# Eight weight loads instead of eleven, the last twelve row blocks of a projection multiplied straight into the next stage's layout, and two closing copies without a shared bank: one decode step of attention and MLP on one core

## The chip, the cores and the metric

The kernel runs on one core of one Trainium2 chip. The metric is the time of one execution in microseconds of device time; the time before is the median of three runs, 190.84 us (190.77 to 190.88). One more execution was recorded by the hardware profiler, and all views of the profile come from that one.

## What is computed

One token passes through two layers. The reference, cut to what matters here:

```
h  = x + A(layernorm(x), k_cache, v_cache, wq, wo)     # x: 1x1x512
out = h + B(layernorm(h), w1, w2, w3, w4)

A: q = x @ wq                       # 32 query heads of 128, 8 key/value heads, 16384 cached positions
   p = softmax(q k^T / sqrt(128));  o = p v;  return o.reshape(1, 1, 4096) @ wo     # wo: 4096x512
B: h = gelu(layernorm(x) @ w1), shifted along the sequence by one or two places, @ w2
   x1 = x + hs                      # with one token the shifted h is all zeros: x1 = x
   return x1 + gelu(layernorm(x1) @ w3) @ w4            # w3: 512x1792, w4: 1792x512
```

Everything is bfloat16. The cache is 64 MB of keys and values, and wq, wo, w3 and w4 are another 11.9 MB; w1 and w2 don't matter, since the shifted branch is zero for a sequence of one.

## The kernel before, in words

The program is written as a list of operations with the tiles that each reads and writes (class Program); semaphore waits follow from that list. Besides, an operation may name a PSUM bank (argument `bank`): then it waits for the last user of that bank on any other engine, even where no data passes between them (line 63). Instructions of one engine keep the order in which they are written.

**The attention** (lines 665 to 682) goes through four pairs of key/value heads. For each pair SyncE issues two loads of 4 MB of keys into the two halves of tile kb and one load of 8 MB of values into vb (two of 4 MB for the last pair). VectorE transposes the keys, TensorE multiplies them with the query, VectorE, ScalarE and TensorE do the softmax, and TensorE multiplies with the values (line 636), four column groups of 32 side by side. The result of a pair is 32 rows of tile o_m.

**The weights behind it** (lines 685 to 693) are loaded by the same SyncE queue in pieces, each with a semaphore of its own. The lists WO, W3 and W4 (lines 329 to 332) say which blocks go together: wo's 32 row blocks in four loads, w3's four in three, w4's fourteen in four. wo goes into the first half of kb, w3 and w4 into the second, so the loads are issued when the last keys there have been transposed, and lie in the queue behind the last values.

**The stages behind the attention** are one chain:

- Lines 696 and 698 (VectorE): o_m is summed into o_f and cast to o_b, 128 partitions by 32 row blocks. The cast waits for the first load of wo.
- Line 702 (TensorE): 32 matmuls, one for each row block of wo, 512 columns each. Four of them run side by side in four column groups of the array and add up in one bank, so the result is four partial rows of 512, each copied over 32 partitions.
- Line 706 (VectorE): the copy osum of that bank into SBUF. Line 708 (TensorE): four fp32 matmuls (two passes each) add up the four partial rows and put quarter q of the row on partitions 32q to 32q+31. This is the "row's layout": four quarters of 128 values, each copied on 32 partitions.
- row_sums (lines 479 to 495): line 483 adds the residual x, held in tile hx since the start, and takes the sum; line 489 the sum of squares, line 491 the transposed row, line 493 (TensorE) the mean over the partitions, line 495 copies it to st.
- Line 714 (ScalarE): hc, the row less its mean in bfloat16. It also waits for the first load of w3.
- Line 720 (TensorE): 16 matmuls with w3. variance (lines 497 to 511), line 724 and line 725 meanwhile give the scales and xsum, the residual of the second layer.
- Lines 729 and 733: for each half of the 14 blocks, the gelu (ScalarE) and a transpose into hcol (VectorE).
- Lines 737 to 751 (TensorE): 14 blocks m of w4, four matmuls each, side by side, all into one bank. In the middle (line 740) four fp32 matmuls with an identity add xsum. A block waits for its load and its half of hcol.
- Line 752 (ScalarE) copies partitions 0 to 63 of the result into fin, line 754 (VectorE) partitions 64 to 127; both name the bank "mn". SyncE sends the row out (line 755) and waits for it (line 757).

**Branches**: TensorE's program is kept short: loops run over the pairs and pieces (method _tensor), and behind them the instructions stand in a row. `pe(None)` and `dve(None)` mark a place where the program branches on a condition that is never true (lines 150 and 314), with a prefetch hint given at the program's start. In the kernel before, TensorE's stands ahead of block 10 of w4.

Of the kernel before, what the change touches and what calls it, by code (L numbers as in the profile page):

```python
# [9 lines left out]
ALU = mybir.AluOpType  # L10
# [308 lines left out]
D = 512  # L319
# [6 lines left out]
NCH = D // 128  # L326
FQ = FM // 4
NHC = FM // 128
WO = ((0, 12), (12, 24), (24, 30), (30, 32))
VP = 2  # L330
W3 = ((0, 2), (2, 3), (3, 4))
W4 = ((0, 5), (5, 10), (10, 13), (13, 14))
BLOCK = (0, 2, 1, 3)
PAIRS = HKV // 2
RPARTS = 9
# [7 lines left out]
def bass_sequential_preLN__gqa_block_cached__mixer_s_mlp__decode_kernel(  # L343
# [13 lines left out]
    with ExitStack() as ctx:  # L357
# [16 lines left out]
        x4 = sb("x4", [4, 128], BF16)  # L374
        mean4 = sb("mean4", [128, 128], FP32)
        ident_f = sb("ident_f", [128, 128], FP32)
        ident = sb("ident", [4, 4], BF16)
        quarter = sb("quarter", [4, 4, 32], BF16)
# [23 lines left out]
        osum = sb("osum", [128, D], FP32)  # L402
# [3 lines left out]
        o_b = sb("o_b", [128, 32], BF16)  # L406
        hr = sb("hr", [128, 128], FP32)
        hx = sb("hx", [128, 128], FP32)
        rs = [sb(f"rs{i}", [128, 2], FP32) for i in range(2)]
        hc = sb("hc", [128, NCH, 32], BF16)  # L410
        xs = sb("xs", [128, 128], FP32)
        xsum = sb("xsum", [128, 128], FP32)
# [3 lines left out]
        fin = sb("fin", [64, 256], BF16)  # L416
# [4 lines left out]
        wq_sb, wo_sb = vb, kb[0]  # L421
# [3 lines left out]
        banks = ps("banks", [128, 8, 512], FP32)  # L425
        s_ps = banks[:, 0:2, :]
        row = banks[:, :, :].rearrange("p b f -> p (b f)")
        O_ps = [banks[:, 2, :], banks[:, 3, :]]
        A_ps, mn_ps = banks[:, 4, :], banks[:, 5, :]
        m_ps, n_ps = mn_ps[:, 0:256], mn_ps[:, 256:512]  # L430


        def load(name, dst, src, key, by="SP", also=()):
            P.op(by, lambda e: e.dma_start(dst, src), w=[key, *also], dma=name)  # L434
# [24 lines left out]
        def dve(fn, r=(), w=(), bank=()):  # L459
            return P.op("DVE", fn, r, w, bank)  # L460

        def act(fn, r=(), w=(), bank=()):
            return P.op("ACT", fn, r, w, bank)
# [4 lines left out]
        def pe(fn, r=(), w=(), bank=(), also=()):  # L468

            return P.op("PE", fn, r, w, bank, also=also)  # L470

        def piece(cuts, m):
            return [lo <= m < hi for lo, hi in cuts].index(True)

        def copies(col, n):

            return col.to_broadcast([col.shape[0], n])

        def row_sums(i, row, key):

            h, hk = (hr, "hr") if i else (hx, "hx")
            if i:
                dve(lambda e: e.scalar_tensor_tensor(h[:, :], row[:, 0:128], 1.0, hx[:, :], ALU.mult, ALU.add,
                                                     accum_out=rs[i][:, 0:1]),
                    r=[key, "hx"], w=[hk, ("rs", i, 0)], bank=[key])
            else:
                dve(lambda e: e.tensor_scalar(h[:, :], row[:, 0:128], 0.0, 0.0, ALU.add, ALU.add,
                                              accum_out=rs[i][:, 0:1]), r=[key], w=[hk, ("rs", i, 0)], bank=[key])
            dve(lambda e: e.scalar_tensor_tensor(xs[:, :], h[:, :], 1.0, h[:, :], ALU.mult, ALU.mult,
                                                 accum_out=rs[i][:, 1:2]), r=[hk], w=["xs", ("rs", i, 1)])  # L490
            dve(lambda e: e.transpose(hT[:, :, :].rearrange("p k u -> p (k u)"),
                                      h[:, :].rearrange("p (i k) -> p k i", k=NCH)), r=[hk], w=["hT"])
            pe(lambda e: e.matmul(n_ps[:, 0:2], mean4[:, :], rs[i][:, :], start=True, stop=True),
               r=[("rs", i, 0), ("rs", i, 1), "mean4"], w=["n"], bank=["mn"])
            dve(lambda e: e.tensor_copy(st[i][:, 0:2], n_ps[:, 0:2]), r=["n"], w=[(("st", i), 0)], bank=["mn"])

        def variance(i):
# [7 lines left out]
            for n in range(1 + i):  # L505
# [22 lines left out]
            r=["ident", "x4"], w=["quarter"])  # L528
        pe(lambda e: e.matmul(O_ps[0][:, 0:128], quarter[:, :, :].rearrange("p q u -> p (q u)"), x4[:, :],
                              start=True, stop=True), r=["quarter"], w=[("O", 0)], bank=[("O", 0)])  # L530
        row_sums(0, O_ps[0], ("O", 0))
        variance(0)
        act(lambda e: e.activation(scr[0:1, 0:1], mean4[0:1, 0:1], ACTF.Exp), r=["mean4"], w=["scr"])
# [4 lines left out]
            r=["ident_f"], w=["row32"])  # L538
        dve(lambda e: e.tensor_reduce(maskdd[:, :], ident_f[:, :].rearrange("p (n d) -> p d n", d=4), AX.X, ALU.add),
            r=["ident_f"], w=["maskdd"])  # L540
# [6 lines left out]
        for z, m, key, mk in ((zo, rowgh, "zo", "rowgh"), (zd, maskgh, "zd", "maskgh")):  # L547
# [5 lines left out]
            r=["hT", (("st", 0), 0), (("st", 0), 6)] + [("v", x) for x in range(VP)], w=["xn"])  # L553
# [3 lines left out]
        for i, key in enumerate(keys):  # L557
            P.part("query", i)
            for k in range(NCH):
                pe(lambda e, k=k: e.matmul(row[:, bass.ds(P.b, 512)], copies(xn[:, k:k + 1], 128),  # L560
                                           wq_k[:, k, bass.ds(P.c, REP * DH)], start=(k == 0), stop=(k == NCH - 1)),
                   r=["xn"], also=[("v", x) for x in range(VP)], w=["n" if key == "mn" else key], bank=[key])
        P.part()
        for g in range(2):
            half = banks[64 * g:64 * g + 64, PAIRS * g:PAIRS * g + PAIRS, :].rearrange("p j c -> p (j c)")
            for b in range(2):
# [3 lines left out]
                    r=["n" if x == "mn" else x for x in keys[PAIRS * g:PAIRS * g + PAIRS]], w=["qcol"],  # L570
                    bank=keys[PAIRS * g:PAIRS * g + PAIRS])
# [112 lines left out]
        act(lambda e: e.activation(scr[0:1, 1:2], mean4[0:1, 0:1], ACTF.Gelu_apprx_tanh), r=["mean4"], w=["scr"])  # L684
        for n, (lo, hi) in enumerate(WO):
            load(f"wo{n}", wo_sb[:, lo * D:hi * D], A_wo.rearrange("(p r) c -> p (r c)", p=128)[:, lo * D:hi * D],
                 ("r", 0, n))
        w3_in = B_w3.rearrange("(p k) f -> p k f", p=128)
        for n, (lo, hi) in enumerate(W3):
            load(f"w3{n}", w3_sb[:, lo:hi, :], w3_in[:, lo:hi, :], ("r", 1, n))  # L690
        w4_in = B_w4.rearrange("(p m) c -> p m c", p=128)
        for n, (lo, hi) in enumerate(W4):
            load(f"w4{n}", w4_sb[:, lo:hi, :], w4_in[:, lo:hi, :], ("r", 1, len(W3) + n))


        dve(lambda e: e.tensor_reduce(o_f[:, :], o_m[:, :, :].rearrange("p d r -> p r d"), AX.X, ALU.add),
            r=["o_m"], w=["o_f"])
        dve(lambda e: e.tensor_copy(o_b[:, :], o_f[:, :]), r=["o_f", ("r", 0, 0)], w=["o_b"])

        for r_ in range(32):  # L700
            q = r_ % 4
            pe(lambda e, r_=r_, q=q: e.matmul(O_ps[0][32 * q:32 * q + 32, :], copies(o_b[:, r_:r_ + 1], 32),  # L702
                                              wo_sb[:, r_ * D:(r_ + 1) * D], start=(r_ < 4), stop=(r_ >= 28)),
               r=["o_b"] + [("r", 0, n) for n in (piece(WO, r_),) if n], w=[("O", 0)], bank=[("O", 0)])
        h_ps, hkey = banks[:, 6, :], "spare0"
        dve(lambda e: e.tensor_copy(osum[:, :], O_ps[0][:, :]), r=[("O", 0)], w=["osum"], bank=[("O", 0)])
        for q in range(4):
            pe(lambda e, q=q: e.matmul(h_ps[32 * q:32 * q + 32, 0:128], copies(row32[:, 0:1], 32),
                                       osum[:, q * 128:(q + 1) * 128], start=True, stop=True),
               r=["osum", "row32"], w=[hkey], bank=[hkey])  # L710
        s = st[1]
        S = ("st", 1)
        row_sums(1, h_ps, hkey)
        act(lambda e: e.activation(hc[:, :, :], hT[:, :, :], ACTF.Identity, bias=s[:, 0:1], scale=1.0),
            r=["hT", (S, 0)] + [("r", 1, 0)], w=["hc"])


        for k in range(NCH):
            for q in range(4):
                pe(lambda e, k=k, q=q: e.matmul(s_ps[32 * q:32 * q + 32, 0, 0:FQ], hc[:, k, :],  # L720
                                                w3_sb[:, k, q * FQ:(q + 1) * FQ], start=(k == 0), stop=(k == NCH - 1)),
                   r=["hc"] + [("r", 1, n) for n in (piece(W3, k),) if n], w=[("s", 0)], bank=[("s", 0)])
        variance(1)
        dve(lambda e: e.tensor_scalar(xs[:, :], hr[:, :], s[:, 0:1], None, ALU.add), r=["hr", (S, 0)], w=["xs"])
        dve(lambda e: e.scalar_tensor_tensor(xsum[:, :], xs[:, :], s[:, 6:7], hr[:, :], ALU.mult, ALU.add),
            r=["hr", "xs", (S, 6)], w=["xsum"])
        for n in range(2):
# [6 lines left out]
                hcol[:, lo:hi, :].rearrange("p m u -> p (m u)"),  # L734
                hg[:, :].rearrange("p (i m) -> p m i", m=NHC)[:, lo:hi, :]), r=[("hg", n)], w=[("hcol", n)])
        dve(None)
        for m in range(NHC):
            if m == NHC // 2:
                for o in range(4):
                    pe(lambda e, o=o: e.matmul(  # L740
                        n_ps[32 * o:32 * o + 32, 0:128], ident_f[:, 32 * BLOCK[o]:32 * BLOCK[o] + 32], xsum[:, :],
                        start=False, stop=False, skip_group_check=True),
                       r=["ident_f", "xsum"], w=["n"], bank=["mn"])
            if m == W4[-2][0]:
                pe(None)
            for o in range(4):
                pe(lambda e, m=m, o=o: e.matmul(  # L747
                    n_ps[32 * o:32 * o + 32, 0:128], hcol[:, m, :], w4_sb[:, m, BLOCK[o] * 128:(BLOCK[o] + 1) * 128],
                    start=(m == 0), stop=(m == NHC - 1),
                    skip_group_check=True),  # L750
                   r=[("hcol", 2 * m // NHC), ("r", 1, len(W3) + piece(W4, m))], w=["n"], bank=["mn"])
        act(lambda e: e.activation(fin[:, 0:128], n_ps[0:64, 0:128], ACTF.Identity),  # L752
            r=["n"], w=[("fin", 0)], bank=["mn"])
        dve(lambda e: e.tensor_copy(fin[:, 128:256], n_ps[64:128, 0:128]), r=["n"], w=[("fin", 1)], bank=["mn"])  # L754
        P.op("SP", lambda e: e.dma_start(out[0, 0:1, :].rearrange("o (q j) -> (o q) j", q=2), fin[31:33, :]),
             r=[("fin", 0), ("fin", 1)], w=["out"], dma="out")
        P.op("SP", lambda e: e.nop(), r=["out"])
# [31 lines left out]
```

## Time and profile before

| | |
|---|---|
| median of three runs | 190.84 us (190.77 to 190.88) |
| the profiled execution's own time | 191.29 us |
| its span, first to last instruction | 189.7 us |
| mean granted TensorE clock | 0.823 |
| busy: TensorE matmuls, weight loads, VectorE, ScalarE, GpSimd | 116.1, 45.8, 115.4, 9.3, 5.7 us |
| read from HBM | 79.17 MB, 417 GB/s over the span |

The span leaves out 1.6 us around the program's instructions. In the profile PE is TensorE's matmuls, PEld its weight loads, DVE VectorE, ACT ScalarE, POOL GpSimd, SP SyncE; a name with q (SPq) is an instruction of the engine's sequencer, such as the issue of a DMA. Times in the views are microseconds from the span's start. "128*32 128x512" means a weight of 128 rows and 32 columns against 512 moving columns.

### The profile page before, as it was taken

What the parts mean: (1) busy time and instruction counts of PE and PEld (TensorE: products, weight loads), DVE (VectorE), ACT (ScalarE), POOL (GpSimd) and SP (SyncE); (2) the same over time, 40 slices, a digit from 0 to 9 for tenths busy, and PEclk for the clock granted to TensorE, in tenths of its full rate; (3) what the DMA queues carried; (4) which work ended last, traced back from release to release, by engine and by line L of the source; (5) the groups of instructions that cost most, each with busy time, mean ns of one, the idle gap of its engine ahead of it and who ended that gap; (6) DMA issues with size and microseconds to landing.
All of it is one profiled execution on the core that took longest, in us unless ns stands there. A gap on an engine that the chain in (4) does not pass through costs nothing.

```text
span 189.7 us, 2177 instructions
## 1 busy us (share of the span) xinstructions
PE 116.1 (61%) x701; PEld 45.8 (24%) x701; DVE 115.4 (61%) x140; ACT 9.3 (5%) x16; POOL 5.7 (3%) x10
## 2 busy tenths in 40 slices
PE   1009709997194498950842999606539996094544
PEld 1004203442031143320310343202213432041113
DVE  4900799995514998945047989460469896604151
ACT  3000000000200000002000000020000000500020
POOL 1900000000000000000000000000000000000010
PEclk9999985999858589995597599975975999759955
DMA  6999999999899999997999998999999999999992
GB/s 221 442 435 442 442 442 449 442 442 442 380 435 408 435 553 428 442 442 339 435 428 422 477 401 387 442 442 435 442 442 442 428 428 415 422 402 416 411 411 106
DMA packets 3613, 79.19 MB, mean 417 GB/s; under 512 B 410, under 2 KB 540, under 8 KB 1564
## 3 DMA queue, kind: packets, MB, share of 16 engines
q1 hardware_dynamic: 3604, 79.17, 97.5%
q8 instruction: 1, 0.02, 0.0%
q10 hardware_dynamic: 8, 0.00, 0.0%
HBM read 79.17 MB, written 0.00 MB: 417 GB/s over the span
## 4 chain that ended last, share of the span: by engine, by line
DMA 66%; DVE 15%; PE 14%; issue 3%; SPq 1%; ACT 0%; DVEq 0%
DMA kb<-in_A_k_cache_dram 46%; DMA kb<-in_B_w_dram 14%; DVE kt L583 13%; PE banks L600 8%; DMA vb<-in_A_wq_dram 7%; PE banks L560 4%; SPq L434 1%; DVE qcol L567 1%; PE banks L594 1%; PE banks L747 1%; DVE qb L574 0%; PE banks L740 0%; DVE xn L551 0%; DVE fin L754 0%; ACT fin L752 0%
## 5 line engine op out<-in xcount | busy, mean ns | idle before, releaser
L583 DVE STREAM_TRANSPOSE kt<-kb 128x2048 int32<-128x2048 int32 (+1 forms) x37 | 71.3, 1988 | 5.8 <-DMA kb<-in_A_k_cache_dram 4.2
L600 PE MATMUL banks<-kt,qn 128*128 x256 | 69.8, 422 | 0.2
L600 PEld LDWEIGHTS banks<-kt,qn 128*128 x256 | 26.6, 104 | 41.9 <-issue 25.1
L636 PE MATMUL banks<-vb,pt 128*32 128x512 bf16 x256 | 22.8, 534 | 2.8 <-POOLq L449 2.8
L652 DVE TENSOR_SCALAR od<-banks,rowc 128x128 f32<-128x128 f32 x4 | 1.4, 351 | 24.7 <-PE banks L636 24.7
L594 PE MATMUL banks<-qn 128*128 128x512 bf16 x8 | 3.9, 494 | 18.4 <-DVE kt L583 18.4
L560 PE MATMUL banks<-vb,xn 128*128 x32 | 8.4, 428 | 10.1 <-DVE xn L551 10.1
L625 DVE STREAM_TRANSPOSE pt<-p_sb 64x1024 bf16<-64x1024 bf16 x8 | 9.9, 1239 | 5.4 <-ACT p_sb L621 5.3
L636 PEld LDWEIGHTS banks<-vb,pt 128*32 128x32 bf16 x256 | 8.6, 130 | 15.2 <-issue 10.3
L621 ACT ACTIVATE p_sb<-banks,bias 128x1024 bf16<-128x1024 f32 x4 | 4.5, 1114 | 155.8 <-DVE nmh L617 155.8
L643 PE MATMUL banks<-acc,zd 128*32 128x1 f32 x8 | 1.1, 203 | 17.7 <-DVE pt L625 17.7
L610 DVE TENSOR_REDUCE mx<-banks 128x1 f32<-128x1024 f32 x4 | 4.9, 1224 | 8.1 <-PE banks L600 8.1
L567 DVE STREAM_TRANSPOSE qcol<-banks 64x1024 f32<-64x1024 f32 x4 | 4.8, 1226 | 6.4 <-PE banks L560 6.4
L560 PEld LDWEIGHTS banks<-vb,xn 128*128 128x128 bf16 x32 | 3.5, 108 | 14.6 <-issue 11.8
L509 POOL TENSOR_TENSOR st<-st,expo 128x1 f32<-128x1 f32 (+1 forms) x2 | 1.3, 630 | 176.1 <-DVE st L507 176.1
L613 PE MATMUL banks<-mxd,mean 128*128 128x128 f32 x8 | 2.0, 326 | 6.6 <-DVE mxd L611 6.6
L594 PEld LDWEIGHTS banks<-qn 128*128 128x128 bf16 x8 | 0.8, 100 | 20.8 <-issue 20.5
L658 PE MATMUL banks<-od,zo 128*32 128x128 f32 x8 | 1.6, 284 | 6.5 <-DVE od L655 6.5
L643 PEld LDWEIGHTS banks<-acc,zd 128*32 128x32 f32 x8 | 0.7, 140 | 18.4 <-DVE pt L625 18.4
L655 DVE SCALAR_TENSOR_TENSOR od<-banks,rowc,od 128x128 f32<-128x128 f32 x12 | 4.2, 351 | 0.4
L702 PE MATMUL banks<-kb,o_b 128*32 128x512 bf16 x32 | 2.7, 384 | 2.4 <-DMA kb<-in_A_wo_dram 1.3
L548 DVE COPY zo<-rowgh 128x32 f32<-128x32 f32 x1 | 3.6, 3627 | 0.0
(71 smaller groups left out, 42.4 us busy)
## 6 DMA issues: line engine op xcount, KB each, us to landing
kb<-in_A_k_cache_dram SPq DMA_DIRECT2D x8, 4096.0 KB, 29.7
vb<-in_A_v_cache_dram SPq DMA_DIRECT2D x2, 4096.0 KB, 29.6
vb<-in_A_wq_dram SPq DMA_DIRECT2D x1, 4096.0 KB, 12.6
kb<-in_A_wo_dram SPq DMA_DIRECT2D x2, 1536.0 KB, 25.4
kb<-in_B_w_dram SPq DMA_DIRECT2D x2, 640.0 KB, 25.4
kb<-in_B_w_dram SPq DMA_DIRECT2D x1, 896.0 KB, 22.4
kb<-in_B_w_dram SPq DMA_DIRECT2D x2, 448.0 KB, 23.4
kb<-in_A_wo_dram SPq DMA_DIRECT2D x1, 768.0 KB, 28.5
```

Of the source, the lines that this page charges most:

```text
L548: dve(lambda e, z=z, m=m: e.tensor_copy(z[:, :].rearrange("p (n d) -> p n d", d=4), m[:, :, :].rearrange("p g h -> p (g h)").unsqueeze(2). ...
L560: pe(lambda e, k=k: e.matmul(row[:, bass.ds(P.b, 512)], copies(xn[:, k:k + 1], 128), wq_k[:, k, bass.ds(P.c, REP * DH)], start=(k == 0), s ...
L567: dve(lambda e, g=g, b=b, half=half: e.transpose(qcol[64 * g:64 * g + 64, 2 * b:2 * b + 2, :, :].rearrange("p e m u -> p (e m u)"), half.r ...
L583: P.op("DVE", lambda e, view=view: e.transpose(view(kt), view(kb[y])), r=[("r", y, i) for i in range(RPARTS)], w=[("kt", t + i) for i in r ...
L594: pe(lambda e: e.matmul(row[:, bass.ds(P.y, 512)], copies(none, 128), copies(none, 512), start=True, stop=False, skip_group_check=True), r ...
L600: pe(lambda e, n=n: e.matmul(row[:, bass.ds(P.y, 512)], qn[:, n, bass.ds(P.q, 128)], key_piece(P.k, n), start=False, stop=(n == 3), skip_g ...
L610: dve(lambda e: e.tensor_reduce(mx[:, :], s_all, AX.X, ALU.max), r=[("s", 0), ("s", 1)], w=["mx"], **both)
L621: act(lambda e: e.activation(p_sb[:, :], s_all, ACTF.Exp, bias=bias[:, 0:1], scale=float(SCALE), accum_out=acc[:, :]), r=[("s", 0), ("s", ...
L625: dve(lambda e, g=g: e.transpose(pt[64 * g:64 * g + 64, :, :, g, :], p_sb[64 * g:64 * g + 64, :]), r=["p"], w=["pt"])
L636: pe(lambda e, l=l, ct=ct, ch=ch: e.matmul(O_ps[0][32 * ct:32 * ct + 32, :], pt[:, l, ch, :, :].rearrange("p g u -> p (g u)"), tiles[:, l ...
L655: dve(lambda e, block=block, c=c: e.scalar_tensor_tensor(od[:, :], block, rowc[:, c:c + 1], od[:, :], ALU.mult, ALU.add), r=[key, "rowc", ...
L702: pe(lambda e, r_=r_, q=q: e.matmul(O_ps[0][32 * q:32 * q + 32, :], copies(o_b[:, r_:r_ + 1], 32), wo_sb[:, r_ * D:(r_ + 1) * D], start=(r ...
```

## The change

- WO, W3 and W4 are cut into three, two and three loads: eight in place of eleven. The first load of wo holds 20 row blocks, the first of w3 three of its four, the first of w4 eight of fourteen.
- Only the first 20 row blocks (`near`) are multiplied by line 702's form and go through osum. The other twelve are multiplied straight into the row's layout: four matmuls of 128 columns each (function direct), one for each quarter, into the bank where osum's four partial rows are added.
- The residual x enters that bank first, by one matmul with `quarter` and x4, as at the start of the kernel; row_sums no longer adds hx.
- The four fp32 matmuls with xsum come ahead of block 0 of w4 instead of block 7.
- TensorE's branch moves from block 10 to block 13.
- Line 754's copy no longer names the bank.

```
-WO = ((0, 12), (12, 24), (24, 30), (30, 32))
+WO = ((0, 20), (20, 28), (28, 32))
...
-W3 = ((0, 2), (2, 3), (3, 4))
-W4 = ((0, 5), (5, 10), (10, 13), (13, 14))
+W3 = ((0, 3), (3, 4))
+W4 = ((0, 8), (8, 13), (13, 14))
...
-            if i:
-                dve(lambda e: e.scalar_tensor_tensor(h[:, :], row[:, 0:128], 1.0, hx[:, :], ALU.mult, ALU.add,
-                                                     accum_out=rs[i][:, 0:1]),
-                    r=[key, "hx"], w=[hk, ("rs", i, 0)], bank=[key])
-            else:
-                dve(lambda e: e.tensor_scalar(h[:, :], row[:, 0:128], 0.0, 0.0, ALU.add, ALU.add,
-                                              accum_out=rs[i][:, 0:1]), r=[key], w=[hk, ("rs", i, 0)], bank=[key])
+            dve(lambda e: e.tensor_scalar(h[:, :], row[:, 0:128], 0.0, 0.0, ALU.add, ALU.add,
+                                          accum_out=rs[i][:, 0:1]), r=[key], w=[hk, ("rs", i, 0)], bank=[key])
...
-        for r_ in range(32):
+        h_ps, hkey = banks[:, 6, :], "spare0"
+        near = WO[0][1]
+        for r_ in range(near):
             q = r_ % 4
             pe(lambda e, r_=r_, q=q: e.matmul(O_ps[0][32 * q:32 * q + 32, :], copies(o_b[:, r_:r_ + 1], 32),
-                                              wo_sb[:, r_ * D:(r_ + 1) * D], start=(r_ < 4), stop=(r_ >= 28)),
-               r=["o_b"] + [("r", 0, n) for n in (piece(WO, r_),) if n], w=[("O", 0)], bank=[("O", 0)])
-        h_ps, hkey = banks[:, 6, :], "spare0"
+                                              wo_sb[:, r_ * D:(r_ + 1) * D], start=(r_ < 4), stop=(r_ >= near - 4)),
+               r=["o_b"], w=[("O", 0)], bank=[("O", 0)])
         dve(lambda e: e.tensor_copy(osum[:, :], O_ps[0][:, :]), r=[("O", 0)], w=["osum"], bank=[("O", 0)])
+        pe(lambda e: e.matmul(h_ps[:, 0:128], quarter[:, :, :].rearrange("p q u -> p (q u)"), x4[:, :],
+                              start=True, stop=False, skip_group_check=True), r=["quarter"], w=[hkey], bank=[hkey])
+
+        def direct(r_):
+            for q in range(4):
+                pe(lambda e, q=q: e.matmul(
+                    h_ps[32 * q:32 * q + 32, 0:128], copies(o_b[:, r_:r_ + 1], 32),
+                    wo_sb[:, r_ * D + q * 128:r_ * D + (q + 1) * 128], start=False, stop=(r_ == 31),
+                    skip_group_check=True),
+                   r=["o_b", ("r", 0, piece(WO, r_))], w=[hkey], bank=[hkey])
+
         for q in range(4):
             pe(lambda e, q=q: e.matmul(h_ps[32 * q:32 * q + 32, 0:128], copies(row32[:, 0:1], 32),
-                                       osum[:, q * 128:(q + 1) * 128], start=True, stop=True),
+                                       osum[:, q * 128:(q + 1) * 128], start=False, stop=False,
+                                       skip_group_check=True),
                r=["osum", "row32"], w=[hkey], bank=[hkey])
+        for r_ in range(near, 32):
+            direct(r_)
...
+        for o in range(4):
+            pe(lambda e, o=o: e.matmul(
+                n_ps[32 * o:32 * o + 32, 0:128], ident_f[:, 32 * BLOCK[o]:32 * BLOCK[o] + 32], xsum[:, :],
+                start=True, stop=False, skip_group_check=True),
+               r=["ident_f", "xsum"], w=["n"], bank=["mn"])
         for m in range(NHC):
-            if m == NHC // 2:
-                for o in range(4):
-                    pe(lambda e, o=o: e.matmul(
-                        n_ps[32 * o:32 * o + 32, 0:128], ident_f[:, 32 * BLOCK[o]:32 * BLOCK[o] + 32], xsum[:, :],
-                        start=False, stop=False, skip_group_check=True),
-                       r=["ident_f", "xsum"], w=["n"], bank=["mn"])
-            if m == W4[-2][0]:
+            if m == W4[-1][0]:
                 pe(None)
...
-        dve(lambda e: e.tensor_copy(fin[:, 128:256], n_ps[64:128, 0:128]), r=["n"], w=[("fin", 1)], bank=["mn"])
+        dve(lambda e: e.tensor_copy(fin[:, 128:256], n_ps[64:128, 0:128]), r=["n"], w=[("fin", 1)])
```

More of the change, by code (lines that the diff above doesn't have):

```diff
@@ L748, in bass_sequential_preLN__gqa_block_cached__mixer_s_mlp__decode_kernel @@
                     n_ps[32 * o:32 * o + 32, 0:128], hcol[:, m, :], w4_sb[:, m, BLOCK[o] * 128:(BLOCK[o] + 1) * 128],
-                    start=(m == 0), stop=(m == NHC - 1),
+                    start=False, stop=(m == NHC - 1),
                     skip_group_check=True),
```

## The prediction

> **What bounds the kernel now.** I read the page's slices first, then the chain of waits by time, then the listing of DMA issues (in short windows, one load at a time), then the timeline of the last 16 us. The page:
>
> ```profile
> PEclk9999985999858589995597599975975999759955
> DMA  6999999999899999997999998999999999999992
> ```
>
> The DMA engines are busy in all slices but the first and the last: the kernel is a stream of 79 MB, and a change behind the attention can win only at the stream's length or behind its end. The chain of waits (start, us, what) shows the end:
>
> ```profile
> 160.12 25.99 DMA kb<-in_B_w_dram
> ...
> 187.78 0.28 ACT fin L752
> ...
> 188.16 0.29 DVE fin L754
> ```
>
> A load of w4 until 186.11, then matmuls, then two copies one behind the other. Issue times (timeline of SyncE) and times to landing (DMA issues) of single loads, each row from its own window:
>
> ```profile
> 133.28 0.33 SPq L434 DMA_DIRECT2D vb<-in_A_v_cache_dram  x1
> vb<-in_A_v_cache_dram SPq DMA_DIRECT2D x1, 4096.0 KB, 25.5
> 134.95 0.33 SPq L434 DMA_DIRECT2D vb<-in_A_v_cache_dram  x1
> vb<-in_A_v_cache_dram SPq DMA_DIRECT2D x1, 4096.0 KB, 33.6
> 149.76 0.43 SPq L434 DMA_DIRECT2D kb<-in_A_wo_dram  x1
> kb<-in_A_wo_dram SPq DMA_DIRECT2D x1, 256.0 KB, 28.7
> 158.70 0.43 SPq L434 DMA_DIRECT2D kb<-in_B_w_dram  x1
> kb<-in_B_w_dram SPq DMA_DIRECT2D x1, 448.0 KB, 23.1
> 159.65 0.43 SPq L434 DMA_DIRECT2D kb<-in_B_w_dram  x1
> kb<-in_B_w_dram SPq DMA_DIRECT2D x1, 640.0 KB, 24.9
> 166.01 3.17 SPq L434 DMA_DIRECT2D kb<-in_B_w_dram  x1
> kb<-in_B_w_dram SPq DMA_DIRECT2D x1, 384.0 KB, 21.1
> 169.22 0.43 SPq L434 DMA_DIRECT2D kb<-in_B_w_dram  x1
> kb<-in_B_w_dram SPq DMA_DIRECT2D x1, 128.0 KB, 18.2
> ```
>
> So the last two loads of values land at 158.78 and 168.55, all of wo at 178.46, w3's third block at 181.8, w4's fifth at 184.55, its tenth at 186.1 (chain), its thirteenth at 187.1 and its last at 187.42. The timeline between:
>
> ```profile
> 174.69 0.18 DVE L698 CAST o_b<-o_f 128x32 bf16<-128x32 f32 x1
> 174.93 0.83 PE L702 MATMUL banks<-kb,o_b 128*32 128x512 bf16 x12 [1.05 <-DVE o_b L698]
> 178.95 0.69 DVE L706 COPY osum<-banks 128x512 f32<-128x512 f32 x1 [4.08 <-PE banks L702]
> 179.69 0.43 PE L708 MATMUL banks<-osum,row 128*32 128x128 f32 x8 [0.79 <-DVE osum L706]
> 180.19 0.29 DVE L483 SCALAR_TENSOR_TENSOR hr<-banks,hx 128x128 f32<-128x128 f32 x1 [0.55 <-PE banks L708]
> 181.70 0.40 ACT L714 ACTIVATE hc<-hT,st 128x128 bf16<-128x128 f32 x1 [16.75 <-DVE st L495]
> 182.15 1.68 PE L720 MATMUL banks<-kb,hc 128*32 128x448 bf16 x16 [0.69 <-ACT hc L714]
> 185.05 0.73 PE L747 MATMUL banks<-kb,hcol 128*32 128x128 bf16 x20 [1.21 <-DVE hcol L733]
> 186.34 0.65 PE L740 MATMUL banks<-xsum,ident_f 128*32 128x128 f32 x8
> 187.10 0.63 PE L747 MATMUL banks<-kb,hcol 128*32 128x128 bf16 x16
> 187.43 0.30 PE L747 MATMUL banks<-kb,hcol 128*32 128x128 bf16 x4
> 188.52 0.33 SPq L755 DMA_DIRECT2D out_dram<-fin  x1
> ```
>
> Block 10 of w4 starts at 187.10 (the row with 16 matmuls, to 187.73) and block 13 at 187.43, each as its load lands. The end is the stream's, plus 0.30 for the last block, the two copies and the way out.
>
> **Part by part.**
>
> *Three loads fewer.* 4096 KB of values take 9.77 us in one load (158.78 to 168.55); wo's 4096 KB take 9.91 in four, 0.05 for each load more. The 3584 KB behind take 8.96 in seven, or 10.24 for 4096 KB in eight: 0.08 for each load more than wo's. Three fewer save 0.15 to 0.24; bounds: nothing, if the time goes by something else than the count, and 0.24. I take 0.18. Nothing is issued earlier that matters: the last issue, at 169.22, stands 18 us before its landing. So w4's thirteenth block, last of its load before and after, lands at 187.06 (block 10's start less the 0.04 that osum's copy takes to follow TensorE) - 0.18 = 186.88, and the last block at 187.24.
>
> *The first loads are larger.* o_b waits for 20 blocks of wo instead of 12: 168.55 + 20/32 x 9.91 = 174.7, just when VectorE is ready (174.69). Behind the cast VectorE has only osum's copy. hc waits for three blocks of w3: 181.8 less two loads' worth, 0.13, is 181.7, just where ScalarE starts it now. Behind hc stand the gelus, which need its product anyway. w4's first eight blocks land at 184.55 + 3/5 x 1.56 - 0.15 = 185.35, where block 0 starts at 185.05 now.
>
> *The direct blocks.* Twelve matmuls of 512 columns last 0.83, three rounds of four side by side: pitch about 0.22 at the full clock, so 0.055 for 128 columns. The 20 near blocks are five rounds, 174.93 to 176.2; osum to 176.95; its matmuls to 177.4. Twelve direct rounds, with wo's last load at 178.35 in between, end at 178.7; at half clock (the twenty matmuls of w4 take 0.73: a round's 0.30 and four pitches of 0.107) all of it ends at 180.2. row_sums starts at 180.19 now, so the chain there gains between nothing and 1.45 us, and keeps none of it: hc waits for w3's load until 181.7. That is the cover, 1 us deep. The residual's one matmul lies under osum's copy, and row_sums' first operation keeps the 0.29 of line 483; the form that takes its place stands at the start of the kernel:
>
> ```profile
> 2.74 0.29 DVE L487 TENSOR_SCALAR_CACHE_REDUCE hx<-banks 128x128 f32<-128x128 f32 x1 [0.38 <-PE banks L529]
> ```
>
> [...]
>
> *xsum first.* Eight fp32 passes, 0.65 us, leave the stretch between w4's tenth block and the end and go into TensorE's idle time between 183.83 and 185.05; they cost nothing there.
>
> *The end.* Blocks 0 to 7 run from 185.4 to 186.4 (seven pitches and 0.30), before 186.88. Then six rounds are left where four were: 186.88 + 0.04 + 5 x 0.107 + 0.30 = 187.76. Now the matmuls end at 187.73. **So TensorE takes over the end from the stream, and the loads' saving is lost in two more rounds behind the late landing**: +0.03 in sum.
>
> *The copies.* VectorE now waits for ScalarE's copy: it starts at 188.16 though the matmuls ended at 187.73. From the matmuls' end to its own it is 0.72. Without the bank it follows TensorE as osum's copy does: 0.04 + 0.29 = 0.33, -0.39. Bounds: -0.39, and 0 if two engines reading one bank hold each other up; they read different partitions, and no row shows such a pair, so I take the whole. Then SyncE's output is late next, unchanged.
>
> Sum: +0.03 - 0.39 = **-0.36**. The profiled execution would go from 191.29 (span 189.7, 1.6 around it) to 190.93; the median, 0.45 below it, from 190.84 to **190.5**. Own range by the bounds: 190.25 to 190.8.
>
> **Rivals.**
>
> *Slower: TensorE's longer program.* Behind the loops it issues, by the code, 32 + 8 + 2 + 16 + 56 + 8 = 122 matmuls now (fp32 ones count twice), each with a weight load; the change makes them 159, 74 instructions more ahead of the end. A load of code shows once in the whole trace (window 187.0 to 188.5, 40 slices):
>
> ```profile
> DMA  0000000009000000000000000000000000000000
> ...
> q8 instruction: 1, 0.02, 3.9%
> ```
>
> It starts at 187.34, when the weights are through, and takes 3.9% x 16 x 1.5 = 0.94 us. If the program now passes the point up to which its code is at hand, that load comes before the end. Within the stream it holds up one of 16 DMA engines by up to 0.94: +0.3 to +0.9, 190.8 to 191.4. If TensorE runs dry of code behind w4's late load (186.9), it waits for the way to HBM (nothing, to the 1.2 us of the 1 KB output, 188.52 to the span's 189.7) and the 0.94, then for the rounds left, some 0.5: matmuls end at 188.3 to 189.5 instead of 187.76. I take 189.2, nearer the output's row: +1.4, **191.9**. It decides when the branch, now ahead of block 13, lies behind that point. Against it: no wait of TensorE for code shows so far.
>
> [...]
>
> *Faster: the clock.* The windows around the stages:
>
> ```profile
> 177.22:180.63 3.41, 1.43 (x16) 0.37 (x16) 1.10 (x4) 0.00 (x0) 0.00 (x0) 1.00 1.01 411
> 180.64:184.04 3.40, 2.27 (x18) 0.91 (x18) 1.79 (x10) 0.55 (x2) 0.70 (x1) 0.50 1.02 413
> 184.05:187.46 3.41, 2.03 (x64) 1.56 (x64) 1.05 (x2) 0.69 (x2) 0.00 (x0) 0.50 0.66 253
> ```
>
> Granted clock 1.00, then 0.50, 0.50. With more work in the first window it may stay up. If it is up at 186.9, the last rounds cost 0.055, the end is the stream's again (187.24 + 0.04 + about 0.2), 0.3 less: **190.2**.
>
> *The copies don't overlap*: 190.85, no change.
>
> **How the numbers follow.** A measurement of this kernel tells about 0.2%, 0.4 us, from no change: faster is below 190.46, slower above 191.22. Forecast 0.50, split by its own range nearly in half at 190.46 (0.20 faster, 0.30 same). Program too long 0.29, of it 0.04 within 0.2%. Clock 0.10, all faster. Copies 0.06, same; anything else 0.05, slower. Together faster 0.30, same 0.40, slower 0.30. The range, 190.1 to 191.9, takes in the clock's case, the load of code within the stream and half of the waits for code; about 0.17 is left out.
>
> **What would show it.** Line 754 starting beside line 752, 0.05 behind the last matmul (the copies). Eight loads, the last landing near 187.2 (loads). hr written near 179 and hc still at 181.7, now released by w3's DMA (cover). Block 8 starting at 186.9 with 24 matmuls back to back to 187.76 (takeover). Wrong would be: a gap in TensorE between blocks 8 and 13 that no landing explains, or an instruction load ahead of 187 (code); hc later than 181.8; PEclk above 0.50 behind 184.

## The result

The changed kernel takes 191.49 us (median of seven, 191.31 to 191.65) against 190.84 before: a ratio of 1.0033, 95% interval 1.0021 to 1.0045. It is slower by 0.65 us. 190.5 was forecast; the time lies in the range, on the side of the rival that had 0.29.

The profiled execution took 191.44 with a span of 190.0. Its stream of weights began 0.6 us earlier than in the profile before (the last values land at 134.51 + 33.5 = 168.0 instead of 168.55), so stages are compared from that landing on. Its last values and its last weights, issue and time to landing, each row from its own window:

```profile
134.51 0.33 SPq L434 DMA_DIRECT2D vb<-in_A_v_cache_dram  x1
vb<-in_A_v_cache_dram SPq DMA_DIRECT2D x1, 4096.0 KB, 33.5
148.72 0.42 SPq L434 DMA_DIRECT2D kb<-in_A_wo_dram  x1
kb<-in_A_wo_dram SPq DMA_DIRECT2D x1, 512.0 KB, 30.4
159.56 0.43 SPq L434 DMA_DIRECT2D kb<-in_B_w_dram  x1
kb<-in_B_w_dram SPq DMA_DIRECT2D x1, 128.0 KB, 28.3
```

All of wo lands at 179.12, 11.1 us behind the values instead of 9.9; the last weights at 187.86, 19.85 behind them instead of 18.87. With three loads fewer the stream became 1.0 us longer, and it lost that while wo's last loads were under way. The timeline (start, us, engine, line, operation) shows the same from TensorE's side:

```profile
174.50 1.26 PE L699 MATMUL banks<-kb,o_b 128*32 128x512 bf16 x20 [1.06 <-DVE o_b L693]
...
176.80 0.63 PE L708 MATMUL banks<-kb,o_b 128*32 128x128 bf16 x32
...
179.17 0.41 PE L708 MATMUL banks<-kb,o_b 128*32 128x128 bf16 x16 [1.74 <-DMA kb<-in_A_wo_dram]
179.62 0.29 DVE L482 TENSOR_SCALAR_CACHE_REDUCE hr<-banks 128x128 f32<-128x128 f32 x1 [3.12 <-PE banks L708]
...
182.48 0.40 ACT L724 ACTIVATE hc<-hT,st 128x128 bf16<-128x128 f32 x1 [18.11 <-DMA kb<-in_B_w_dram]
...
187.58 0.83 PE L756 MATMUL banks<-kb,hcol 128*32 128x128 bf16 x24 [0.41 <-DMA kb<-in_B_w_dram]
188.46 0.27 ACT L761 ACTIVATE fin<-banks 64x128 bf16<-64x128 f32 x1 [2.94 <-PE banks L756]
188.46 0.29 DVE L763 CAST fin<-banks 64x128 bf16<-64x128 f32 x1 [2.24 <-PE banks L756]
```

Everything behind is as forecast, only later: hc is released by w3's DMA, six rounds of w4 run back to back for 0.83 us, and the two copies start together. In between, TensorE waits 1.74 us for wo's last load. What lies there is in the DMA queues. In the window 174.6 to 176.7 the queues' list holds only the weights:

```profile
q1 hardware_dynamic: 163, 0.86, 99.7%
```

and in the window 176.75 to 177.95

```profile
q1 hardware_dynamic: 85, 0.51, 103.6%
q8 instruction: 1, 0.02, 5.6%
```

The one load of code, at 187.34 before, now comes at 176.8, in the middle of the stream, and takes 5.6% x 16 x 1.2 = 1.08 us.

The trace shows where that time goes. Each load of weights sends sixteen signals as its parts land, and what waits for the load goes on with the last of them. Of wo's last load fifteen signals come from 177.60 to 177.82 and one at 179.12; of w3's first load fifteen come up to 181.06 and one at 182.40, and hc starts at 182.48; of the last weights fifteen come up to 186.59 and one at 187.87. The sixteenth is 1.3 us behind the others in all loads that land behind the load of code. In the change's first two loads of wo, which land ahead of that (174.07 and 176.57), it is 0.03 and 0.05 behind, in the kernel before 0.45, in run 5 below, where the load of code comes late, 0.05. So one part in sixteen of the stream is held up, and every load behind waits for it.

### The profile page after: what moved, and what is told of

The parts are those of the page before. It is cut to its first block, busy times and chain, and to the rows that moved or that the text cites. A ratio compares the mean times of both kernels' runs of the same rounds, so it can differ in the third digit from the quotient of the medians.

```text
span 190.0 us, 2248 instructions
## 1 busy us (share of the span) xinstructions
PE 115.5 (61%) x738; PEld 46.5 (24%) x738; DVE 115.4 (61%) x140; ACT 9.3 (5%) x16; POOL 5.7 (3%) x10
## 4 chain that ended last, share of the span: by engine, by line
DMA 67%; DVE 15%; PE 14%; issue 2%; SPq 1%; DVEq 0%
DMA kb<-in_A_k_cache_dram 45%; DMA kb<-in_B_w_dram 15%; DVE kt L578 14%; PE banks L595 8%; DMA vb<-in_A_wq_dram 6%; PE banks L555 4%; DVE qcol L562 1%; PE banks L589 1%; SPq L434 1%; PE banks L756 0%; DVE qb L569 0%; DVE xn L546 0%; DVE fin L763 0%; DVEq L137 0%; SPq L137 0%
## 5 line engine op out<-in xcount | busy, mean ns | idle before, releaser
L595 PE MATMUL banks<-kt,qn 128*128 x256 | 68.8, 417 | 0.2
L543 DVE COPY zd<-maskgh 128x32 f32<-128x32 f32 x1 | 3.6, 3555 | 0.0
```

The costliest lines, as they stand in the source:

```text
L543: dve(lambda e, z=z, m=m: e.tensor_copy(z[:, :].rearrange("p (n d) -> p n d", d=4), m[:, :, :].rearrange("p g h -> p (g h)").unsqueeze(2). ...
L595: pe(lambda e, n=n: e.matmul(row[:, bass.ds(P.y, 512)], qn[:, n, bass.ds(P.q, 128)], key_piece(P.k, n), start=False, stop=(n == 3), skip_g ...
```

## Experiments: what brings the load of code

My theory was that TensorE's program became too long ("length") or its branch moved too far back ("place"); the rivals were that the larger loads are slower or that the direct matmuls disturb the stream. The load of code is found in the DMA queues' list (q8); the code at hand is what TensorE can run without a further load. That code comes in pieces, as the expectations of runs 1 and 5 have it, was my assumption: the list shows one load of 0.02 MB within the span, and no run shows where a piece ends.

**1. The branch alone.** The changed kernel, with the branch four blocks of w4 earlier:

```
-            if m == W4[-1][0]:
+            if m == 9:
                 pe(None)
```

> The changed kernel with TensorE's never-taken branch ahead of block 9 of w4 instead of block 13, nothing else. Theory (place of the branch): the hinted branch holds back the load of TensorE's next piece of code until it is passed, but only if it stands in the piece of code that TensorE is entering; four blocks earlier (32 instructions) it does, so the instruction load moves from 176.8 us to behind 187.5, the weights are not held up, and the time is the 190.5 that was forecast (0.6 above to nothing above 190.45). Rival (length): TensorE's added 74 instructions bring the load wherever the branch stands: the load stays near 176.8 and the time 191.4 to 191.6.

191.44 us, the same as the change (1.0037 of before, 1.0023 to 1.0051). The load of code stays early, in the window 176.4 to 177.6:

```profile
q1 hardware_dynamic: 109, 0.54, 110.4%
q8 instruction: 1, 0.02, 5.6%
```

By that, length looked right and place wrong; the place had only not been moved far enough, as run 5 shows.

**2. The kernel before, made as long.** No part of the change but the branch, and TensorE's program as long as the changed one's:

```
+            if r_ == 23:
+                for _ in range(37):
+                    pe(lambda e: e.matmul(banks[0:32, 7, 0:8], copies(o_b[:, 0:1], 32), wo_sb[:, 0:8],
+                                          start=True, stop=True), r=["o_b"], w=["spare1"], bank=["spare1"])
...
-            if m == W4[-2][0]:
+            if m == W4[-1][0]:
```

> The kernel before with 37 added matmuls of 8 columns into an unused bank, written behind row block 23 of the projection, where TensorE waits for the next load, and with the branch ahead of block 13 as in the changed kernel: TensorE's program then has the changed kernel's length and the branch stands at the same instruction, and nothing else is changed. They are results that nobody reads. If the code alone makes the loss, the instruction load comes near 177 and the time is 1.0 to 1.3 above before, 191.8 to 192.1. If the loss comes from the loads' cut or the direct matmuls, the time is before's, 190.8 to 191.0.

191.84 against 190.91, 1.0046 (1.0032 to 1.0059). The load of code comes at 176.4 here too (window 176.3 to 177.5), the added matmuls lie in a wait as intended, and wo's third load, which they cannot touch, is late. It lands 10.7 us behind the values; in the kernel before, whose row comes first, 9.3:

```profile
177.86 1.05 PE L702 MATMUL banks<-kb,o_b 128*32 128x512 bf16 x8 [1.07 <-DMA kb<-in_A_wo_dram]
...
q8 instruction: 1, 0.02, 5.1%
...
176.57 1.18 PE L707 MATMUL banks<-kb,o_b 128*32 128x8 bf16 x37
178.85 1.28 PE L702 MATMUL banks<-kb,o_b 128*32 128x512 bf16 x8 [1.11 <-DMA kb<-in_A_wo_dram]
```

Without the new cut of the loads and without the direct matmuls, the longer program with its later branch costs 0.9 us, somewhat less than the 1.0 to 1.3 expected. The two rivals are out as its cause.

**3. The change without the direct blocks**, 72 instructions shorter:

```
-        near = WO[0][1]
+        near = 32
```

(with the waits of the old form for the later loads).

> The changed kernel with all 32 row blocks of the projection in the old form, no direct blocks; eight loads, residual first, xsum first, copies without the bank and the branch at block 13 stay. TensorE's program is 72 instructions shorter than the changed kernel's. Both theories on the code expect the instruction load behind 187 again and 190.4 to 190.6. If the loss came from the larger loads themselves (fewer, larger pieces being slower) the last of wo would still land 1.2 us late and the time stay above 191.2.

192.25 us, 1.0070 (1.0056 to 1.0084), though the span is only 188.7: both theories missed. The last load of wo lands 9.9 us behind the values, so the larger loads are not slow. The load of code is out of the stream again, as expected, but comes at 188.4, when the work is all but done (window 188 to 190):

```profile
DMA  0000000900000000000000000000000000000000
...
q8 instruction: 1, 0.02, 3.3%
```

It is through at 188.4 + 3.3% x 16 x 2 = 189.45, and the profiled execution's own time is 191.89: 3.2 us lie behind the span's end instead of 1.6. So I added to the theory that a late load holds up the program's end. Some 0.3 of the short span is the clock's: from 186 to 188 the granted clock is 1.00 here and 0.50 in the change, and the last six rounds of w4 take 0.53 instead of 0.83.

**4. The branch later in the kernel before**, ahead of block 13, nothing else:

```
-            if m == W4[-2][0]:
+            if m == W4[-1][0]:
```

> The kernel before with the branch ahead of block 13 instead of block 10, nothing else. It is passed once the load of blocks 10 to 12 has landed, about 0.8 us later. If code loaded too late holds up what follows the span, the instruction load moves to 188.0 to 188.5, the span stays at 189.3 to 189.7, and the time rises by 0.5 to 1.3, to 191.4 to 192.2. If the load of code behind the weights is free whenever it comes: 190.9, no change.

193.36 us in the middle, with a wide spread: the six executions took 190.97, 191.37, 193.34, 193.39, 194.14 and 194.16 against 190.87, so one line costs 0.1 to 2.5 us in the first four and 3.3 in the last two (ratio 1.0126, 1.0086 to 1.0167). The spans of all six are 189.3 to 189.5, as before the edit (189.2 to 189.6): what is lost lies behind the span, where 1.6, 2.0, 3.8 and 4.1 us pass in the first four, 4.7 in the last two, instead of 1.4 to 1.7. The profile shows a load of code 0.5 later than before (187.87), but it is of the fastest execution, 190.97. What the others waited for, no profile shows.

**5. The branch far earlier in the changed kernel**, ahead of block 0:

```
-            if m == W4[-1][0]:
+            if m == 0:
```

> The changed kernel with the branch ahead of block 0 of w4, 104 instructions earlier than in the change. Place of the branch: it now stands well inside TensorE's second piece of code, so the load is held back until it is passed, near 185.4, and starts near 186.5; 191.0 to 191.6, since it then falls into the last weights or the matmuls wait for their code. Length: the program reaches into a third piece of code whatever stands where, and the load stays at 176.4 to 176.8; 191.4 to 191.5 as the change.

193.13 us, 1.0130 (1.0108 to 1.0153): longer than both theories said, but the load of code is where the place of the branch puts it, at 186.1, and the stream is whole. From the values' landing to the last weights':

```profile
134.97 0.33 SPq L434 DMA_DIRECT2D vb<-in_A_v_cache_dram  x1
vb<-in_A_v_cache_dram SPq DMA_DIRECT2D x1, 4096.0 KB, 33.2
159.80 0.43 SPq L434 DMA_DIRECT2D kb<-in_B_w_dram  x1
kb<-in_B_w_dram SPq DMA_DIRECT2D x1, 128.0 KB, 27.0
```

18.65 us (168.15 to 186.8), 1.2 less than in the change with the same instructions and loads. The time is lost elsewhere, in TensorE:

```profile
185.05 0.80 PE L756 MATMUL banks<-kb,hcol 128*32 128x128 bf16 x21 [0.81 <-DMA kb<-in_B_w_dram]
188.46 1.15 PE L756 MATMUL banks<-kb,hcol 128*32 128x128 bf16 x35 [2.60 <-issue]
```

After 21 of w4's 56 matmuls it stops for 2.6 us, released by nothing that the profile knows ("issue"), though the next blocks came with the load of block 0. 35 matmuls, 70 instructions, lie behind the stop. By my count of the code, good to an instruction or two, the program has 533 instructions, so what is at hand ends near instruction 463. The kernel before has 459: it fits by about four. The 461 of run 3's kernel fit too.

**6. Four matmuls too many.** That number can be tested: run 2's edit with `range(4)` in the kernel before, its branch left ahead of block 10.

> The kernel before with four added matmuls of 8 columns into an unused bank behind row block 23, where TensorE waits anyway (results that nobody reads); the branch stays ahead of block 10. In the run with the branch ahead of block 0 TensorE ran dry after 21 matmuls of w4, which puts the limit of the code at hand four instructions behind the end of the kernel before. Theory: four matmuls more (8 instructions) push the last two matmuls over that limit while the branch stays in front of it; so the load still comes near 187.3, is through at 188.3, and the last two matmuls wait for it: they end at 188.6 to 189.8 instead of 187.7, time 191.9 to 193.2. Rival (the length counts only as busy time): 190.8 to 191.0.

193.31 against 190.82, 1.0127 (1.0110 to 1.0144). The load of code (window 187 to 189) and the end of w4 in the timeline:

```profile
q8 instruction: 1, 0.02, 3.9%
...
186.55 0.97 PE L751 MATMUL banks<-kb,hcol 128*32 128x128 bf16 x26
189.96 0.29 PE L751 MATMUL banks<-kb,hcol 128*32 128x128 bf16 x2 [2.44 <-issue]
```

The last two matmuls, as counted, stand still for 2.44 us. Four matmuls of 8 columns in idle time cost 2.5 us of the kernel. The last two end at 190.25, later than the 188.6 to 189.8 expected: TensorE goes on 1.3 to 1.4 us after the load is through (here 187.3 + 3.9% x 16 x 2 = 188.55 to 189.96, in run 5 187.1 to 188.46), which I had not counted. The trace's own rows say the same without my count: behind the loops TensorE runs exactly 251 instructions before it stops, in run 5 and here. The kernel before has 246 there, run 3's kernel 249.

By my count the branch stands at instruction 523 in the change and in run 2, at 491 in run 1, and there the load came in the stream; it stands at 451 in run 3, 449 in run 4, 425 in the kernel before and 419 in run 5, and there it came behind the branch. So the hinted branch held the load back in each run where it stands within the code at hand, and in none where it stands behind it: place and length look like one condition. Nothing between 451 and 491 was tried, and no run is without the branch.

## Experiments: the parts without the code

**7. The copies alone.**

```
-        dve(lambda e: e.tensor_copy(fin[:, 128:256], n_ps[64:128, 0:128]), r=["n"], w=[("fin", 1)], bank=["mn"])
+        dve(lambda e: e.tensor_copy(fin[:, 128:256], n_ps[64:128, 0:128]), r=["n"], w=[("fin", 1)])
```

> The kernel before with only the bank taken off the last copy. Both closing copies start together behind the last matmul: 0.36 to 0.39 less than before, 190.45 to 190.5. The rival that two engines reading one bank hold each other up expects 190.8.

190.56 against 190.91, 0.9982 (0.9973 to 0.9991): 0.35 less. Both copies start together and keep their length:

```profile
187.46 0.27 ACT L752 ACTIVATE fin<-banks 64x128 bf16<-64x128 f32 x1 [2.98 <-PE banks L747]
187.46 0.29 DVE L754 CAST fin<-banks 64x128 bf16<-64x128 f32 x1 [2.26 <-PE banks L747]
```

**8. The loads alone**, with w4 cut at 10 and 13:

```
+WO = ((0, 20), (20, 28), (28, 32))
...
+W3 = ((0, 3), (3, 4))
+W4 = ((0, 10), (10, 13), (13, 14))
```

> The kernel before with wo in three loads (20, 8, 4 blocks), w3 in two (3, 1) and w4 in three (10, 3, 1): eight loads, everything else as before, the branch ahead of block 10. By the prediction's step the stream ends 0.15 to 0.24 earlier, and since as many blocks are left behind the late loads as before, the time falls by 0.1 to 0.24: 190.67 to 190.8. If larger first loads cost more than they save (o_b, hc or block 0 later): 190.9 to 191.1.

191.31 against 190.87, 1.0024 (1.0015 to 1.0033): slower by 0.44. The stream did get shorter, but block 0 of w4 waits for the tenth (185.64), where the kernel before has five blocks done by 185.8:

```profile
185.64 0.94 PE L747 MATMUL banks<-kb,hcol 128*32 128x128 bf16 x28 [2.12 <-DMA kb<-in_B_w_dram]
186.34 0.66 PE L740 MATMUL banks<-xsum,ident_f 128*32 128x128 f32 x8
186.77 0.98 PE L747 MATMUL banks<-kb,hcol 128*32 128x128 bf16 x28
```

TensorE then runs without a gap to 187.75, xsum's 0.65 in the middle: the takeover that the prediction named, at a larger price.

**9. All near, branch with block 10.** Run 3's kernel with this w4 cut and the branch where the kernel before has it.

```
-W4 = ((0, 8), (8, 13), (13, 14))
+W4 = ((0, 10), (10, 13), (13, 14))
...
-            if m == W4[-1][0]:
+            if m == W4[-2][0]:
```

> The kernel of the run with all 32 row blocks near, with w4 cut at blocks 10 and 13 instead of 8 and 13 and the branch ahead of block 10, where the kernel before has it. Theory (a window for the load of code): code is loaded once, some 1.1 to 1.7 us behind the branch; it must come behind the weights and be through before TensorE has to leave the program. With the branch released by block 10's load the instruction load starts within 187.0 to 187.5, span and time lie 1.1 to 1.6 apart as before, and the time is 190.2 to 190.5, the shortest so far. Rival (what follows the span in the all-near run has another cause, such as the shorter first bank group): the time stays at 192.

190.98, 1.0009 (1.0001 to 1.0018): 1.3 less than run 3, not the 190.2 to 190.5 expected. The load of code comes at 187.3, and 1.8 us (190.89 - 189.1) lie behind the span of the profiled execution. The end comes 2.4 us behind the load's end (188.5), as in run 3. That the end is held by the load is not shown by this: the profiled execution of run 4 ended 2.2 behind its load, with no more than 1.6 behind its span.

**10. All near, branch ahead of block 8.** Run 3's kernel with one line:

```
-            if m == W4[-1][0]:
+            if m == 8:
```

> The all-near kernel (the change without the direct blocks) with the branch ahead of block 8 instead of block 13, nothing else. Theory (one load of code, bound to the branch; too early it holds up the weights, too late the end of the program, which comes no sooner than 2.4 us behind it): the branch is passed 1.6 us earlier, once w4's first eight blocks have landed, the load starts near 186.2 and is through by 187.3, so the span's 188.7 and 1.5 behind it count: 190.1 to 190.4, shorter than before and than the copies alone. If the load holds up the last weights there: 190.8 to 191.4. Rival (something else in the all-near run keeps the end): 192 again.

190.35 against 191.00, 0.9965 (0.9950 to 0.9979), as the theory had it. The load of code comes at 186.4 (window 186.3 to 187.5), under the last landings, and they are not late: 135.26 + 32.9 to 159.75 + 27.0, 18.6 us.

Against run 3 this is one line and 1.9 us. The spans of the executions are much the same, 188.7 to 189.2 there and 188.9 to 189.1 here; behind them lie 3.1 to 3.5 us there and 1.3 to 1.4 here. So the place of the branch set what lies behind the span here.

```profile
DMA  0009000000000000000000000000000000000000
...
q8 instruction: 1, 0.02, 5.0%
```

```profile
135.26 0.33 SPq L434 DMA_DIRECT2D vb<-in_A_v_cache_dram  x1
vb<-in_A_v_cache_dram SPq DMA_DIRECT2D x1, 4096.0 KB, 32.9
159.75 0.43 SPq L434 DMA_DIRECT2D kb<-in_B_w_dram  x1
kb<-in_B_w_dram SPq DMA_DIRECT2D x1, 128.0 KB, 27.0
```

**11 and 12. Nine loads**: run 3's kernel with w4 in the four loads of before, and the branch ahead of block 10, then of block 5.

```
+W4 = ((0, 5), (5, 10), (10, 13), (13, 14))
...
-            if m == W4[-1][0]:
+            if m == 10:
```

> The all-near kernel with w4 in the four loads of before (nine loads in all) and the branch ahead of block 10. TensorE has five blocks done before the late loads, as before, and the stream is two loads shorter: matmuls end 0.1 to 0.2 earlier than in the kernel before, the copies give 0.36, the load of code comes near 187.3: 190.3 to 190.5 if it is the span that counts, 190.6 to 190.9 if the code load's end plus 2.4 does.

190.54, 0.9976 (0.9966 to 0.9987), between the two cases; the profiled execution has 2.0 us behind its span of 188.6.

> The same nine loads with the branch ahead of block 5, passed 0.5 to 1 us earlier. If the end of the program waits for the load of code: 0.2 to 0.5 less than the run with branch 10. If the span counts: the same. If the load falls into the last weights: the last landing 0.3 to 1.2 later and the time above 190.9.

**190.18**, 0.9958 (0.9944 to 0.9972): 0.36 less than with block 10, as expected if the end waits for code, with 1.3 us behind the span. This is the fastest version: 0.8 us below the kernel before and 1.3 below the change: the change without its direct blocks, with w4 in four loads and the branch ahead of block 5.

## Why the prediction was wrong, point by point

- **Eight loads**: right. The stream from the values to the last weights is 18.6 us in runs 5 and 10, 18.87 before: 0.2 to 0.3 saved, 0.18 forecast. In the change the load of code hides that.
- **The cover behind the projection**: hc is released by w3's DMA, as forecast, but at 182.48, for w3 is late as well. hr is written 11.6 us behind the values, as before, since wo's last load is late. No run shows hr near 179: in run 5, with the stream whole, the granted clock is 0.50 there and hr comes 11.8 behind the values, the lower end of the forecast, no gain. The fastest version has no direct blocks; no run has them with the load of code out of the way of stream and TensorE alike, so what they alone are worth stays open.
- **xsum first, TensorE takes over the end**: right in place and size. Six rounds behind w4's thirteenth block take 0.83 (forecast 5 x 0.107 + 0.30), at a granted clock of 0.50 from 185 to 188: the rival of the faster clock did not come. Run 8 shows what the takeover costs when w4's first load is larger still.
- **The copies**: right, -0.35 measured alone against -0.39.
- **The step that failed is the sum**: the line "+0.03 - 0.39 = -0.36" takes the stream's end from the number of loads alone, the direct blocks' instructions at nothing. The 74 of them move the load of code from 187.34 to 176.8, and the stream ends 1.2 us later than with the same loads and the code held back (19.85 against 18.65 in run 5). Two of the prediction's own signs of being wrong came: a load of code ahead of 187, and hc later than 181.8. -0.36 + 1.2 is +0.8; measured is +0.65. The rest is about the 0.2 by which less lies behind the span (1.4 in the profiled execution of the change, 1.6 before). The other terms hold: run 10, with the same loads, copies and order of xsum but without direct blocks, has spans 0.4 shorter than the kernel before (189.0 against 189.4, medians).
- **The rival was named, priced too low and held too unlikely.** It had the mechanism, the load of code within the stream, but its price, "+0.3 to +0.9", ended at the load's own length of 0.94. Where the point lies up to which code is at hand, the trace before did not show; by my count runs 3, 5 and 6 put it between 461 and 467 instructions. In the middle of the stream the delay was no shorter than the load: the last weights are 1.2 late in the change, 1.0 in run 1 and 1.4 in run 2. That the time still fell into the stated range is owed to this rival, not to the sum. Its other form, TensorE out of code (191.9), did not occur in the change, whose load of code came at 176.8 and which shows no such stop; runs 5 and 6 show it at 193.1 to 193.3.
- **The branch** was costed at nothing in the sum. Its place decided when code was loaded (188.4 in run 3, 186.4 in run 10): run 4 moves it alone, and loses 0.1 to 2.5 us in four of six executions, and run 10 takes 1.9 less than run 3.

What stays open: what starts the early load at 176.4 to 176.8, how far behind the branch the held-back load begins (1.0 to 1.7 us in most runs here, 2.5 in run 5), and the wide spread of run 4. From 186.1 to 186.4, when the stream is nearly through, the load of code held up the last weights by at most 0.2 (run 12; nothing to be seen in runs 5 and 10).

## What to carry to other kernels

In this kernel instructions had a cost of their own once TensorE's program no longer fitted the code at hand (0.9 us in run 2, 2.5 in run 6): count them, and look in the DMA queues' list for when code is loaded before a change adds any. The load of code did best under the end of the stream of weights (run 10, 190.35): not inside it (the change, 191.49), and not so late that the time behind the span grew (run 3, 192.25). And a stage that waits for a later load, as hc does for w3's (182.48 in the change), has nothing to win by being faster.

## What was not expected of the hardware

- A load of 0.02 MB of code inside the stream delayed the last weights by 1.0 to 1.4 us (the change, runs 1 and 2), though it is one packet of 1.08 us in the change. In the change fifteen of the sixteen signals of each load behind it come in time and one 1.3 late, and the load is waited for until that one. Why 1.08 us of code make 1.3 us of delay is not shown.
- TensorE, out of code, went on only 1.3 to 1.4 us after the load was through; with the load itself it stood still for 2.6 us in run 5 and 2.4 in run 6.
- The end of the execution lay 1.3 to 4.1 us behind the span's end, and one line that moves the branch changed it (runs 3, 4 and 10): the span alone would have called run 3 (188.7) one of the fastest.
